# Attention in float32 on one core: two of a chunk's three visits of values' products moved right behind a visit of scores

## Chip, cores, metric

One core of a Trainium2 chip. The metric is the device time of one execution in microseconds (us). Before the change three executions took 698.53, 699.43 and 701.90 us, median 699.43.

## What is computed

```python
# attention: q, k, v are 2 x 12 x 448 x 64 (batch, heads, rows, depth); w_pre, w_post 12 x 12
scores = scale * np.matmul(q, k.transpose(0, 1, 3, 2))
scores = np.einsum('bhij,hg->bgij', scores, w_pre)          # premix over heads
scores = scores - np.max(scores, axis=-1, keepdims=True)
attn = np.exp(scores)
attn = attn / (np.sum(attn, axis=-1, keepdims=True) + 1e-09)
attn = np.einsum('bhij,hg->bgij', attn, w_post)             # postmix over heads
attn_out = np.matmul(attn, v)
# then two feed-forward layers on 896 x 768 tokens (768 -> 2048 -> 768)
g = h * relu6 / 6.0; x = g @ w_out                          # first, h = x @ w_in
g = P / (Q + 1e-06); out = g @ w_out                        # second, P and Q polynomials of h
```

Everything is float32. The two feed-forward layers fill the time from about 225 us on, and the change touches none of their code.

## The kernel before

The 448 query rows of a batch are cut into chunks of 120, 120, 120 and 88 rows (scores are made for 90 of the last), eight chunks over the two batches. A chunk is worked through in **steps** of ten query rows: G = 12 steps in a full chunk, 9 in the last of a batch, 90 steps in all. Counted through, chunk 2 holds steps 24 to 35, chunk 3 holds 36 to 44, chunk 4 holds 45 to 56, chunk 5 holds 57 to 68, chunk 6 holds 69 to 80 and chunk 7 holds 81 to 89. Tiles of a step hold 12 heads times 10 rows on 120 partitions.

Each step m does this:

- `gsplit(m+3)` (L294, L296): GpSimd splits the scores of step m+3 (tile `full`) into a rounded part `sh` and a rest `sl`, three steps ahead.
- `premix(m)` (L306 to L308): three products into bank `M`; VectorE takes the negated maximum (L310), ScalarE the exponential with its row sum (L312).
- `norm`, `weigh` (L320, L321, L325): VectorE takes the reciprocal of the sum, ScalarE scales the postmix weights with it into `wr`. In program order `weigh(m-1)` comes behind the exponential of `premix(m)`, but before it if the step before had a visit (`full_step`).
- `postmix(m-2)` (L341): four products of `e` and `wr` into bank `A`; at the start of the next step ScalarE evacuates them into `at` (L348).

On top of that come **visits** on TensorE. A visit of scores (L271, 12 products, four banks `sc`) makes four heads' scores of the next chunk. Their sums are copied to `stg`, half by ScalarE and half by VectorE (L274), and SyncE spreads them by DMA into `full` (L252), one issue per head. A visit of values' products (`av_unit`, L363, 16 products, one bank `X`) multiplies `at` of the previous chunk with the values `vraw`; its sum goes through ScalarE into `x` or `XH` (L379) and through VectorE into `XL` (L380), and behind a visit SyncE loads the next values into the `vraw` buffers that it freed (L136). A chunk has three visits of either kind. A step without a visit is called a **thin step** below.

The program is recorded in the order of the loop (`tc.manual_schedule`), so each engine runs its instructions in that order. The steps at which visits come are tables: `SST` for scores, `AVST` for values' products.

```python
    SST = {12: [1, 1, 3, 3, 5, 5], 9: [0, 0, 2, 2, 4, 4]}
    AVST = {12: [7, 7, 9, 9, 11, 11], 9: [5, 5, 7, 7, 8, 8]}
            for p in posts[:1] + xposts:
                p[0]()
            gsplit(m + 3)()
            if C:
                for p in posts[:1]:
                    p[1]()
            premix(m)
```

PSUM has two banks `M`, two `A` and four `sc`; bank `X` is one of the four `sc`.

Of the kernel before, what the change touches and what calls it, by code (L numbers as in the profile page):

```python
# [7 lines left out]
F32 = mybir.dt.float32  # L8
# [11 lines left out]
B, H, S, D = 2, 12, 448, 64  # L20
# [28 lines left out]
def fused_kernel(  # L49
# [280 lines left out]
    def postmix(m):  # L330
        C, g = groups[m]
        r, rr = GP, GR
        c0 = row_of(chunks[C], g)
        if g == 0:
            at[C] = att.tile([JP, JC, H, CH], F32, tag="at", bufs=2, name=f"at{C}")
        e, st = epx.pop(m)
        wr = wrs.pop(m)
        A = ps.tile([128, 512], F32, tag="A", name=f"A{m}")
        av = A[:JP, : JC * H * rr].rearrange("p (c h i) -> p c h i", c=JC, h=H)
        for jc in range(JC):  # L340
            nc.tensor.matmul(  # L341
                av[:, jc], lhsT=e[:r, jc * JP : (jc + 1) * JP], rhs=wr[:r, :, :rr], start=True, stop=True
            )
        o = at[C][:, :, :, c0 : c0 + rr]
        if m in BYV:
            aposts.append(lambda: nc.vector.tensor_copy(out=o, in_=av))
        else:
            aposts.append(lambda: nc.scalar.activation(out=o, in_=av, func=AF.Copy))  # L348

    xps = {}  # L350

    def av_unit(C, h):
        b, r0, n, G = chunks[C]
        if h % 2 == 0:
            return
        if h % 4 == 1:
            tag = "sc" if C + 1 < len(chunks) or h == 1 else "A"
            xps[C] = ps.tile([128, 512], F32, tag=tag, bufs=BUFS[tag], name=f"X{C}_{h}")
        X = xps[C][:, : 2 * CH].rearrange("p (h n) -> p h n", n=CH)
        for jc in range(JC):  # L360
            for hh in (h - 1, h):
                vs = vraw[(C, hh // 2)][:, hh % 2, :].rearrange("p (c d) -> p c d", d=D)
                nc.tensor.matmul(  # L363
                    X[hh % 2 * D : hh % 2 * D + D, hh % 4 // 2, :n], lhsT=vs[:, jc, :], rhs=at[C][:, jc, hh, :n],
                    start=(jc == 0), stop=(jc == JC - 1),
                )
        load_v(*((C, h // 2 + 4) if h // 2 + 4 < NP else (C + 1, h // 2 + 4 - NP)))
        if h % 4 == 3:
            av_evac(C, h, X)

    def av_evac(C, h, X):
        b, r0, n, G = chunks[C]
        c0 = (h - 3) // 2
        t0 = b * S + r0
        src = X[:, :, :n]
        cs, ts_ = slice(c0, c0 + 2), slice(t0, t0 + n)
        o = (x1 if t0 < XRAW else XH)[:, cs, ts_]
# [194 lines left out]
    LAG = 2  # L572
    ONES, BYV = [1, 3, 5], (5, 7, 9)


    SST = {12: [1, 1, 3, 3, 5, 5], 9: [0, 0, 2, 2, 4, 4]}
    QST = {12: [8, 9], 9: [6, 7]}
    AVST = {12: [7, 7, 9, 9, 11, 11], 9: [5, 5, 7, 7, 8, 8]}
    VAT = 11
# [6 lines left out]
    for C, (b, r0, n, G) in enumerate(chunks):  # L586
# [6 lines left out]

        sst = SST[G] if C else ONES
        if nxt is not None:
# [9 lines left out]
        if C > 0:  # L605
            add([lambda h=h: av_unit(C - 1, h) for h in range(1, H, 2)], [("av", a) for a in (AVST[G] if nxt is not None else AVLAST)])

        for s in range(G):
# [11 lines left out]
            if full_step:  # L620
                norm(m - 1)
                weigh(m - 1)
            for p in posts[:1] + xposts:
                p[0]()
            gsplit(m + 3)()
            if C:
# [27 lines left out]
            if m >= LAG:  # L654
                postmix(m - LAG)
            for u in sched.get(("av", s), []):
                u()
            for u in sched.get(s, []):
                u()
# [42 lines left out]
    pieces(2)  # L702
    for h in range(1, H, 2):
        av_unit(C, h)
        flush()
# [293 lines left out]
```

## Time and profile before

| | us |
|---|---|
| three executions | 698.53, 699.43, 701.90 |
| the profiled execution | 697.88 |
| span of its profile | 696.1 |
| TensorE busy in it | 686.3 |
| ScalarE busy | 433.8 |
| VectorE busy | 532.7 |
| GpSimd busy | 168.2 |

The profile is of one execution; its span is 1.8 us shorter than its time. Busy times of TensorE are modelled from each product's start, so that products seem to overlap; the distance between starts is the firmer number, and it is used below.

### The profile page before, as it was taken

Reading aid. Unit: us, or ns where it says so; the run is one execution under the profiler, and the core shown is the slowest. Engines: PE = TensorE matmul, PEld = TensorE weight load, DVE = VectorE, ACT = ScalarE, POOL = GpSimd, SP = SyncE. Lnnn points to the kernel's source line nnn. Section 1 sums busy time; section 2 is a strip of 40 time slices with the busy share of each in tenths; the row PEclk is TensorE's granted clock in tenths of the full one; section 3 lists DMA queues with packets and bytes.
Section 4 is the critical chain, followed back from the end, with each engine's and each line's share of the span. In section 5 each row is a group of like instructions: output and inputs, shape, how many; then the busy total and the mean of one; then the engine's idle time right before and its main releaser. Section 6 shows DMA issues by size and latency. Waiting matters only on the chain.

```text
span 696.1 us, 12343 instructions
## 1 busy us (share of the span) xinstructions
PE 686.3 (99%) x4460; PEld 616.2 (89%) x4461; DVE 532.7 (77%) x964; ACT 433.8 (62%) x881; POOL 168.2 (24%) x195
## 2 busy tenths in 40 slices
PE   8999999999999999999999999999999999999998
PEld 4779888888889888989889888898999999999997
DVE  6855685666657699999976556549999899989991
ACT  6767787787887455555543222237766667669851
POOL 2987775877776200000000000000000000000000
PEclk9999999999999999999999999999999999999999
DMA  5646486545394377675743332517666574755522
GB/s 200 232 133 175 138 215 197 163 139 165 120 265 124 113 246 213 199 218 183 230 156 121 121 122 88 184 54 273 212 240 211 180 267 166 243 181 207 190 81 90
DMA packets 76032, 122.81 MB, mean 176 GB/s; under 512 B 6804, under 2 KB 56260, under 8 KB 75972
## 3 DMA queue, kind: packets, MB, share of 16 engines
q1 hardware_dynamic: 75684, 121.66, 54.2%
q8 instruction: 35, 0.57, 0.3%
q10 hardware_dynamic: 288, 0.37, 0.1%
q14 instruction: 25, 0.20, 0.1%
HBM read 83.39 MB, written 19.27 MB: 147 GB/s over the span
## 4 chain that ended last, share of the span: by engine, by line
PE 93%; DMA 2%; DVE 2%; issue 1%; ACT 1%; POOL 0%; SPq 0%; POOLq 0%; DVEq 0%
PE h L389 11%; PE h L388 11%; PE h L387 11%; PE A L341 9%; PE acc L387 6%; PE acc L389 6%; PE acc L388 6%; PE y L388 6%; PE y L387 6%; PE y L389 6%; PE X L363 5%; PE sc L271 4%; PE M L306 3%; PE M L308 2%; PE M L307 2%; DMA vraw<-in_v_dram 1%
## 5 line engine op out<-in xcount | busy, mean ns | idle before, releaser
L389 PE MATMUL h<-xh,wl 128*128 128x512 f32 (+1 forms) x384 | 139.7, 364 | 0.0
L388 PE MATMUL h<-xl,wh 128*128 128x512 f32 (+1 forms) x384 | 139.5, 363 | 0.0
L387 PE MATMUL h<-xh,wh 128*128 128x512 f32 (+1 forms) x384 | 139.5, 363 | 0.0
L296 POOL TENSOR_TENSOR sl<-full,sh 120x448 fp32r<-120x448 f32 x87 | 100.0, 1149 | 7.3
L341 PEld LDWEIGHTS A<-wr,e 120*112 120x112 f32 x720 | 86.4, 176 | 8.0 <-ACT wr L325 4.0
L310 DVE TENSOR_REDUCE st<-M 120x1 f32<-120x448 f32 x90 | 56.0, 622 | 48.2 <-PE M L308 48.1
L341 PE MATMUL A<-wr,e 120*112 120x120 f32 x720 | 88.9, 266 | 2.2 <-ACT wr L325 2.2
L312 ACT ACTIVATE e<-M,st 120x448 f32<-120x448 f32 x90 | 57.1, 635 | 40.5 <-DVE st L310 34.4
L462 ACT ACTIVATE wh<-wf 128x768 fp32r<-128x768 f32 (+1 forms) x52 | 42.6, 819 | 62.0 <-PE y L388 46.6
L387 PEld LDWEIGHTS h<-xh,wh 128*128 128x128 f32 x384 | 72.1, 188 | 7.5
L388 PEld LDWEIGHTS h<-xl,wh 128*128 128x128 f32 x384 | 72.1, 188 | 7.6
L389 PEld LDWEIGHTS h<-xh,wl 128*128 128x128 f32 x384 | 72.1, 188 | 7.6
L435 ACT ACTIVATE wf<-wraw 128x768 f32<-128x768 f32 (+1 forms) x56 | 49.5, 883 | 42.9 <-DVE wl L463 40.8
L463 DVE TENSOR_TENSOR wl<-wf,wh 128x768 fp32r<-128x768 f32 (+1 forms) x52 | 49.6, 954 | 32.4 <-ACT wh L462 32.4
L388 PE MATMUL y<-gl,wh 128*128 128x384 f32 x192 | 70.1, 365 | 0.0
L387 PE MATMUL y<-gh,wh 128*128 128x384 f32 x192 | 69.9, 364 | 0.0
L389 PE MATMUL y<-gh,wl 128*128 128x384 f32 x192 | 69.5, 362 | 0.0
L294 POOL TENSOR_SCALAR sh<-full 120x448 fp32r<-120x448 f32 x87 | 54.0, 620 | 43.5 <-PE M L307 20.6
L443 DVE SCALAR_TENSOR_TENSOR wf<-wraw,icst,wf 128x768 int32<-128x768 int32 (+1 forms) x56 | 56.5, 1011 | 0.7
L439 DVE SCALAR_TENSOR_TENSOR wf<-wraw,icst,wf 128x768 int32<-128x768 int32 (+1 forms) x56 | 55.9, 999 | 0.9
L348 ACT ACTIVATE at<-A 112x480 f32<-112x480 f32 x87 | 50.3, 579 | 1.8 <-PE A L341 1.8
L389 PE MATMUL acc<-ws,xl 128*128 128x384 f32 x128 | 42.8, 334 | 0.0
(115 smaller groups left out, 1416.3 us busy)
## 6 DMA issues: line engine op xcount, KB each, us to landing
wraw<-in_moe_w_out_dram SPq DMA_DIRECT2D x28, 768.0 KB
wraw<-in_moe_w_in_dram SPq DMA_DIRECT2D x22, 768.0 KB
full<-stg SPq DMA_DIRECT2D x60, 210.0 KB
vraw<-in_v_dram SPq DMA_DIRECT2D x42, 224.0 KB
wpre<-in_moe_w_in_dram SPq DMA_DIRECT2D x10, 768.0 KB
w2h<-wh SPq DMA_DIRECT2D x16, 384.0 KB
w2l<-wl SPq DMA_DIRECT2D x16, 384.0 KB
ws<-w2h SPq DMA_DIRECT2D x16, 384.0 KB
```

The source lines that it names most:

```text
L294: eng.tensor_scalar(out=sh[:r], in0=s[:r], scalar1=1.0, scalar2=0.0, op0=ALU.mult, op1=ALU.add)
L296: return lambda: eng.tensor_tensor(out=sl[:r], in0=s[:r], in1=sh[:r].bitcast(F32), op=ALU.subtract)
L310: nc.vector.tensor_reduce(out=st[:r, 0:1], in_=mt[:r, :S], op=ALU.max, axis=AX.X, negate=True)
L312: nc.scalar.activation(out=e[:r], in_=mt[:r, :S], func=AF.Exp, bias=st[:r, 0:1], accum_out=st[:r, 1:2])
L341: nc.tensor.matmul(av[:, jc], lhsT=e[:r, jc * JP : (jc + 1) * JP], rhs=wr[:r, :, :rr], start=True, stop=True)
L348: aposts.append(lambda: nc.scalar.activation(out=o, in_=av, func=AF.Copy))
L387: nc.tensor.matmul(o, lhsT=wh, rhs=mh, start=first, stop=False)
L388: nc.tensor.matmul(o, lhsT=wh, rhs=ml, start=False, stop=False)
L389: nc.tensor.matmul(o, lhsT=wl, rhs=mh, start=False, stop=last)
L439: nc.vector.scalar_tensor_tensor(out=wi, in0=hw, scalar=icst[:, 0:1], in1=wi, op0=ALU.bitwise_and, op1=ALU.bitwise_or)
L443: nc.vector.scalar_tensor_tensor(out=wi, in0=lw, scalar=icst[:, 1:2], in1=wi, op0=ALU.logical_shift_right, op1=ALU.bitwise_or)
L463: nc.vector.tensor_tensor(out=lv, in0=w, in1=hv.bitcast(F32), op=ALU.subtract)
```

## The change

From chunk 2 to chunk 6 (`joint`) the tables change. In a full chunk scores come at steps 1, 3 and 6 (were 1, 3, 5), values' products at 3, 6 and 9 (were 7, 9, 11); in chunk 3, of nine steps, scores stay at 0, 2 and 4 and values' products come at 2, 4 and 7 (were 5, 7, 8). So two of three visits of values' products stand directly behind a visit of scores in the same step (a **joint visit**), and the scores are recorded first there. Their bank is one of the two `A` banks instead of one of the four `sc`. In a joint chunk all copies of scores and of `X`, ScalarE's and VectorE's, are recorded before the step's `premix`. The other edits rename arguments (`hp` for a pair of heads, `wide`) or keep chunks 0, 1 and 7 as they were.

```diff
@@ -342,38 +342,35 @@
                 av[:, jc], lhsT=e[:r, jc * JP : (jc + 1) * JP], rhs=wr[:r, :, :rr], start=True, stop=True
             )
         o = at[C][:, :, :, c0 : c0 + rr]
-        if m in BYV:
+        if (g if C else m) in BYV[C > 0]:
             aposts.append(lambda: nc.vector.tensor_copy(out=o, in_=av))
         else:
             aposts.append(lambda: nc.scalar.activation(out=o, in_=av, func=AF.Copy))
 
     xps = {}
 
-    def av_unit(C, h):
+    def av_unit(C, hp, wide, tag):
         b, r0, n, G = chunks[C]
-        if h % 2 == 0:
-            return
-        if h % 4 == 1:
-            tag = "sc" if C + 1 < len(chunks) or h == 1 else "A"
-            xps[C] = ps.tile([128, 512], F32, tag=tag, bufs=BUFS[tag], name=f"X{C}_{h}")
-        X = xps[C][:, : 2 * CH].rearrange("p (h n) -> p h n", n=CH)
+        i = hp % wide
+        if i == 0:
+            xps[C] = ps.tile([128, 512], F32, tag=tag, bufs=BUFS[tag], name=f"X{C}_{hp}")
+        X = xps[C][:, : wide * CH].rearrange("p (h n) -> p h n", n=CH)
+        vs = vraw[(C, hp)].rearrange("p h (c d) -> p h c d", d=D)
         for jc in range(JC):
-            for hh in (h - 1, h):
-                vs = vraw[(C, hh // 2)][:, hh % 2, :].rearrange("p (c d) -> p c d", d=D)
+            for k in range(2):
                 nc.tensor.matmul(
-                    X[hh % 2 * D : hh % 2 * D + D, hh % 4 // 2, :n], lhsT=vs[:, jc, :], rhs=at[C][:, jc, hh, :n],
+                    X[k * D : k * D + D, i, :n], lhsT=vs[:, k, jc, :], rhs=at[C][:, jc, 2 * hp + k, :n],
                     start=(jc == 0), stop=(jc == JC - 1),
                 )
-        load_v(*((C, h // 2 + 4) if h // 2 + 4 < NP else (C + 1, h // 2 + 4 - NP)))
-        if h % 4 == 3:
-            av_evac(C, h, X)
-
-    def av_evac(C, h, X):
+        load_v(*((C, hp + 4) if hp + 4 < NP else (C + 1, hp + 4 - NP)))
+        if i == wide - 1:
+            av_evac(C, hp - i, hp + 1, X)
+
+    def av_evac(C, p0, p1, X):
         b, r0, n, G = chunks[C]
-        c0 = (h - 3) // 2
         t0 = b * S + r0
         src = X[:, :, :n]
-        cs, ts_ = slice(c0, c0 + 2), slice(t0, t0 + n)
+        cs, ts_ = slice(p0, p1), slice(t0, t0 + n)
         o = (x1 if t0 < XRAW else XH)[:, cs, ts_]
         xposts.append([
             lambda: nc.scalar.activation(out=o, in_=src, func=AF.Copy),
@@ -570,12 +567,14 @@
             aposts.pop(0)()
 
     LAG = 2
-    ONES, BYV = [1, 3, 5], (5, 7, 9)
-
-
-    SST = {12: [1, 1, 3, 3, 5, 5], 9: [0, 0, 2, 2, 4, 4]}
+    ONES, BYV = [1, 3, 5], [(5, 7, 9), ()]
+
+
+    SST = {12: [1, 1, 3, 3, 6, 6], 9: [0, 0, 2, 2, 4, 4]}
+    SST1, AVST1 = [1, 1, 3, 3, 5, 5], [7, 7, 9, 9, 11, 11]
     QST = {12: [8, 9], 9: [6, 7]}
-    AVST = {12: [7, 7, 9, 9, 11, 11], 9: [5, 5, 7, 7, 8, 8]}
+    AVST = {12: [3, 3, 6, 6, 9, 9], 9: [2, 2, 4, 4, 7, 7]}
+    WIDE = 2
     VAT = 11
     AVLAST = [2, 2, 4, 4, 6, 6]
     full_step = False
@@ -591,7 +590,8 @@
             for i, u in enumerate(units):
                 sched.setdefault(steps[i * len(steps) // len(units)], []).append(u)
 
-        sst = SST[G] if C else ONES
+        sst = (ONES, SST1)[C] if C < 2 else SST[G]
+        joint = C > 1 and nxt is not None
         if nxt is not None:
             kw = {} if C else {"first": nc.vector.tensor_copy}
             add([lambda h=h: scores(nxt, h, **kw) for h in range(0 if C else FIRST, NP)], sst)
@@ -603,7 +603,9 @@
         if C == NCH - 1:
             add([lambda h=h: k_prep(1, h) for h in range(4, NP)], [0, 1])
         if C > 0:
-            add([lambda h=h: av_unit(C - 1, h) for h in range(1, H, 2)], [("av", a) for a in (AVST[G] if nxt is not None else AVLAST)])
+            wide = WIDE if joint else 2
+            avst = AVST[G] if joint else AVST1 if nxt is not None else AVLAST
+            add([lambda h=h: av_unit(C - 1, h, wide, "A" if joint else "sc") for h in range(NP)], [("av", a) for a in avst])
 
         for s in range(G):
             if s == (5 if C == 1 else 0) and C and C + 2 < len(chunks):
@@ -620,8 +622,14 @@
             if full_step:
                 norm(m - 1)
                 weigh(m - 1)
-            for p in posts[:1] + xposts:
+            first = posts if joint else posts[:1]
+            for p in first + xposts:
                 p[0]()
+            if joint:
+                for p in first + xposts:
+                    p[1]()
+                posts.clear()
+                xposts.clear()
             gsplit(m + 3)()
             if C:
                 for p in posts[:1]:
@@ -653,9 +661,9 @@
                 next(wpieces)
             if m >= LAG:
                 postmix(m - LAG)
+            for u in sched.get(s, []):
+                u()
             for u in sched.get(("av", s), []):
-                u()
-            for u in sched.get(s, []):
                 u()
             if C == PRE and s == LATE - 1:
                 flush()
@@ -700,8 +708,8 @@
     drain()
     load_units(3)
     pieces(2)
-    for h in range(1, H, 2):
-        av_unit(C, h)
+    for h in range(NP):
+        av_unit(C, h, 2, "sc" if h < 2 else "A")
         flush()
     run(h110)
     h101 = ps.tile([128, 512], F32, tag="M", name="h1_0_1")

```

**TensorE, chunk 2, from the second visit of scores to the third** (`sc` scores, `X` values' products, `M` premix, `A` postmix). Before:

```order
L271 MATMUL sc_7_1181<-xh,qr 90x448
L306 MATMUL M_1202<-sh_1076,wp_h 120x448
L307 MATMUL M_1202<-sh_1076,wp_l 120x448
L308 MATMUL M_1202<-sl_1077,wp_h 120x448
L341 MATMUL A_1214<-wr_1164,e_1135 112x120 x4
L306 MATMUL M_1224<-sh_1123,wp_h 120x448
L307 MATMUL M_1224<-sh_1123,wp_l 120x448
L308 MATMUL M_1224<-sl_1124,wp_h 120x448
L341 MATMUL A_1236<-wr_1192,e_1160 112x120 x4
L271 MATMUL sc_8_1241<-xh,qr 90x448
```

and now, up to the premix of the third step:

```order
L271 MATMUL sc_7_1181<-xh,qr 90x448
L361 MATMUL X_0_1189<-at_720,vraw_0_967 64x120 x8
L361 MATMUL X_0_1189<-at_720,vraw_1_977 64x120 x8
L306 MATMUL M_1229<-sh_1076,wp_h 120x448
L307 MATMUL M_1229<-sh_1076,wp_l 120x448
L308 MATMUL M_1229<-sl_1077,wp_h 120x448
L341 MATMUL A_1237<-wr_1164,e_1139 112x120 x4
L306 MATMUL M_1247<-sh_1129,wp_h 120x448
L307 MATMUL M_1247<-sh_1129,wp_l 120x448
L308 MATMUL M_1247<-sl_1130,wp_h 120x448
L341 MATMUL A_1259<-wr_1213,e_1160 112x120 x4
L306 MATMUL M_1269<-sh_1150,wp_h 120x448
```

The values' products stand behind the scores, and where every second step had a visit, two thin steps now follow each other before the third visit.

**ScalarE, the same place** (`stg` copies of scores, `x` the sum of values' products, `e` exponential, `at` evacuation, `wr` weights). Before:

```order
L274 COPY stg_2_1173<-sc_4_1171 90x448
L312 ACTIVATE e_1208,st_1206<-M_1202,st_1206 120x448
L274 COPY stg_3_1182<-sc_6_1180 90x448
L348 ACTIVATE at_1141<-A_1214 112x48x10
L312 ACTIVATE e_1230,st_1228<-M_1224,st_1228 120x448
L325 ACTIVATE wr_1234<-wq,st_1206 120x120
L348 ACTIVATE at_1141<-A_1236 112x48x10
L325 ACTIVATE wr_1262<-wq,st_1228 120x120
L274 COPY stg_4_1243<-sc_8_1241 90x448
```

and now:

```order
L274 COPY stg_2_1173<-sc_4_1171 90x448
L274 COPY stg_3_1182<-sc_6_1180 90x448
L376 ACTIVATE x_131<-X_0_1189 128x2x120
L312 ACTIVATE e_1235,st_1233<-M_1229,st_1233 120x448
L348 ACTIVATE at_1141<-A_1237 112x48x10
L312 ACTIVATE e_1253,st_1251<-M_1247,st_1251 120x448
L325 ACTIVATE wr_1257<-wq,st_1233 120x120
L348 ACTIVATE at_1141<-A_1259 112x48x10
L312 ACTIVATE e_1275,st_1273<-M_1269,st_1273 120x448
L325 ACTIVATE wr_1279<-wq,st_1251 120x120
L348 ACTIVATE at_1141<-A_1281 112x48x10
L325 ACTIVATE wr_1330<-wq,st_1273 120x120
```

All three copies come ahead of the exponential, and there is one more place at which the weights stand behind the next step's exponential: `wr_1257` behind `e_1253` as `wr_1234` behind `e_1230`, and `wr_1279` behind `e_1275`.

**SyncE, the last spreads of chunk 3** (`full<-stg` spreads one head's scores of chunk 4, `vraw` loads values). Before:

```order
L252 DMA full_1511<-stg_3_1598 10x12x448 x2
L252 DMA full_1511<-stg_4_1660 10x12x448 x2
L252 DMA full_1511<-stg_5_1669 10x12x448 x2
L136 DMA vraw_4_1715<-in_v_dram 112x512
L136 DMA vraw_5_1725<-in_v_dram 112x512
```

and now:

```order
L136 DMA vraw_0_1708<-in_v_dram 112x512
L136 DMA vraw_1_1718<-in_v_dram 112x512
L252 DMA full_1511<-stg_4_1683 10x12x448
L252 DMA full_1511<-stg_5_1692 10x12x448
L252 DMA full_1511<-stg_4_1683 10x12x448
L252 DMA full_1511<-stg_5_1692 10x12x448
L136 DMA vraw_2_1806<-in_v_dram 112x512
```

The four last spreads stand behind two loads of values, which wait for the products of the joint visit.

## Rows read from the trace of the kernel before

**Rows 1.** The page: parts 1 and 2, busy time by engine and TensorE's granted clock.

```profile
PE 686.3 (99%) x4460; PEld 616.2 (89%) x4461; DVE 532.7 (77%) x964; ACT 433.8 (62%) x881; POOL 168.2 (24%) x195
...
PEclk9999999999999999999999999999999999999999
```

**Rows 2.** Timeline of TensorE, steps 57 to 59; start us, us, engine, line, operation.

```profile
145.92 0.46 PE L306 MATMUL M<-sh,wp_h 120*120 120x448 f32 x1
...
146.63 0.98 PE L341 MATMUL A<-wr,e 120*112 120x120 f32 x8
147.38 0.44 PE L306 MATMUL M<-sh,wp_h 120*120 120x448 f32 x1
...
148.05 0.98 PE L341 MATMUL A<-wr,e 120*112 120x120 f32 x8
148.96 0.46 PE L271 MATMUL sc<-xh,qr 64*120 64x448 f32 x2
...
150.07 0.37 PE L271 MATMUL sc<-xh,qr 64*120 64x448 f32 x2
150.37 0.46 PE L306 MATMUL M<-sh,wp_h 120*120 120x448 f32 x1
```

**Rows 3.** Timeline of TensorE, a visit of values' products in chunk 5.

```profile
161.43 0.98 PE L341 MATMUL A<-wr,e 120*112 120x120 f32 x8
162.34 1.86 PE L363 MATMUL X<-at,vraw 112*64 112x120 f32 x32
164.13 0.47 PE L306 MATMUL M<-sh,wp_h 120*120 120x448 f32 x1
```

**Rows 4.** Timeline of ScalarE, step 58: exponential, weights, evacuation, weights.

```profile
148.97 0.64 ACT L312 ACTIVATE e<-M,st 120x448 f32<-120x448 f32 x1 [0.28 <-DVE st L320]
...
149.59 0.38 ACT L325 ACTIVATE wr<-wq,st 120x120 f32<-120x120 f32 x1
...
149.88 0.57 ACT L348 ACTIVATE at<-A 112x480 f32<-112x480 f32 x1
...
150.34 0.38 ACT L325 ACTIVATE wr<-wq,st 120x120 f32<-120x120 f32 x1
```

**Rows 5.** Timeline, step 8 in chunk 0, third of three thin steps in a row.

```profile
30.06 0.37 PE L308 MATMUL M<-sl,wp_h 120*120 120x448 f32 x1
...
30.37 0.38 ACT L325 ACTIVATE wr<-wq,st 120x120 f32<-120x120 f32 x1
...
30.80 1.07 PE L341 MATMUL A<-wr,e 120*112 120x120 f32 x8 [0.38 <-ACT wr L325]
```

**Rows 6.** Timelines of SyncE, TensorE and GpSimd, end of chunk 3.

```profile
110.49 1.61 SPq L252 DMA_DIRECT2D full<-stg  x2
...
114.87 1.13 SPq L136 DMA_DIRECT2D vraw<-in_v_dram  x2
...
115.58 0.18 PEld L306 LDWEIGHTS M<-sh,wp_h 120*120 120x120 f32 x1 [0.16 <-issue]
...
116.86 0.56 POOL L294 TENSOR_SCALAR sh<-full 120x448 fp32r<-120x448 f32 x1 [7.00 <-DMA vraw<-in_v_dram]
...
117.52 1.63 PEld L363 LDWEIGHTS X<-at,vraw 112*64 112x64 f32 x32 [0.44 <-DMA vraw<-in_v_dram]
...
119.48 1.14 POOL L296 TENSOR_TENSOR sl<-full,sh 120x448 fp32r<-120x448 f32 x1
```

**Rows 7.** Timeline, step 36: key conversion on ScalarE, TensorE's wait.

```profile
94.56 1.03 ACT L236 ACTIVATE xh<-kraw 128x448 fp32r<-128x448 f32 x2
...
98.01 0.18 PEld L271 LDWEIGHTS sc<-xh,qr 64*120 64x120 f32 x2 [0.48 <-DVE xh L237]
```

**Rows 8.** Timeline, steps 81 to 83: ScalarE's further work and TensorE's wait.

```profile
201.43 0.90 ACT L435 ACTIVATE wf<-wraw 128x768 f32<-128x768 f32 x1
...
203.81 0.70 ACT L513 CAST xh<-x 128x568 fp32r<-128x568 f32 x1
...
206.27 1.07 PE L341 MATMUL A<-wr,e 120*112 120x120 f32 x8 [0.94 <-ACT wr L325]
```

## Prediction

> **What bounds the kernel now.** I read the page first, then TensorE's own timeline through the 90 steps, then the other engines around it. [...] There [rows 2] a thin step lasts 1.46 us from premix to premix (145.92 to 147.38), of which the postmix takes 0.75 (146.63 to 147.38), and the next step, with a visit of scores, lasts 2.99 (147.38 to 150.37). These two lengths repeat without a wait of TensorE for another engine from step 24 to step 82 except in steps 36 [rows 7] and 44 [rows 6], a step with a visit of values' products being about 0.4 longer. So in the stretch that the change touches TensorE is the bound, and a change there gains only what it takes off TensorE, and loses whatever it makes TensorE wait.
>
> Why does nothing wait? Because thin step and visit alternate. Rows 4 show what the visit covers [rows 4]. In step 58 the exponential starts at 148.97, and only behind it come the weights of step 57, 149.59 to 149.97. That is 2.59 us after the step's premix began (147.38). The postmix that needs them comes after the next premix. With a visit between (148.96 to 150.37 [rows 2]) it comes at about 151.04, 1.1 us after the weights are ready. Without one it would come 2.1 us after that premix (1.46 for the thin step, 0.67 for the premix, 147.38 to 148.05 [rows 2]), half a microsecond too early.
>
> **The change, part by part.**
>
> *Products, copies, loads.* As many as before, on the same engines; only their places move. There are ten joint visits (two in each of chunks 2 to 6).
>
> *Switches of kind on TensorE.* A postmix takes 0.75 us up to a premix but 0.91 up to scores (148.05 to 148.96 [rows 2]) and 0.91 up to values' products (161.43 to 162.34 [rows 3]): 0.16 for entering either kind of visit. Leaving scores costs about 0.10: the last pair of products takes 0.30 to the premix (150.07 to 150.37 [rows 2]), the five pairs before it 0.22 each (148.96 to 150.07). Joining puts one passage from scores to values' products in the place of one leaving and one entering, 0.26 together. No row shows that passage. Its bounds are 0 (saving 0.26) and 0.26 (saving nothing); I take 0.16, as for entering values' products, which is the nearest row. Saving 0.10 each, ten times: **-1.0** (0 to -2.6).
>
> [...]
>
> *Thin steps in a row.* This is the price of joining: the visits no longer alternate. In a full chunk steps 4 and 5, 7 and 8, and 10 and 11 with the next chunk's first are thin in a row. Behind two thin steps the third step's postmix needs weights that stand behind the second's exponential: ready at 2.59 us, wanted at 2.1, so about 0.5 us late. The trace has that very pattern in chunk 0 [rows 5]. The postmix of step 8, third in a row, starts at 30.80, 0.74 after the premix's last product at 30.06, where 0.20 is usual; it is 0.54 late, and the weights (30.37 to 30.75) end just ahead of it. Such steps, apart from the chunks' seams, are 30, 33, 43, 51, 54, 63, 66, 75 and 78: nine times 0.5 is **+4.5** (0.47 to 0.64 each, 4.2 to 5.8).
>
> *The spread of scores at the seams.* Before, scores of chunk 3 were all made by step 40, with four further steps ahead of chunk 4, three of them with a visit. The visits stay there, but the last four spreads now stand behind two loads of values that wait for the joint visit to end, and fewer visits follow. Count from T, the end of that visit. The second load before was issued by 0.4 after the visit (issue ends 116.00, next premix at 115.58 [rows 6]). Four spreads at about 0.85 (two take 1.61, from 110.49 [rows 6]) end at T+3.85. The issue that ended at 112.10 was followed by the split at 116.86, 4.76 later [rows 6]; so `full` is complete at T+8.6. The split takes 0.56 for `sh` and 1.14 for `sl` [rows 6], with 0.1 between, so `sh` is there at T+9.2 and `sl` at T+10.4. TensorE arrives after the steps between. For chunk 4 these are three thin steps and one with values' products (1.45, 1.43, 3.9 with its wait of 0.5, 1.45; 3.4 is 1.46 + 0.16 + 1.79 [rows 2, 3]), T+8.2: 1.0 late at `sh`, then 0.7 at `sl`. For chunk 5 they are four thin ones and a shorter visit, T+9.25: `sl` 0.65 late. For chunk 6, T+9.7, 0.2 late. Then GpSimd needs 1.8 for each further step where thin steps want 1.45, about 0.5 more per seam until a visit comes. Sum 2.2 + 1.15 + 0.7: **+4.1** (2.2, if spreads land a microsecond earlier, to 7.0, if one later). For chunks 3 and 7 the spreads are a quarter smaller and land in time.
>
> *Two seams with other work.* In step 36 TensorE waits 0.48 for key conversions now [rows 7]. Afterwards its postmix is third in a thin run, with one conversion (0.5, half of the 1.03 for two [rows 7]) on ScalarE ahead of the weights: 1.0 late, net **+0.5** (0.3 to 1.0). At steps 81 to 83 ScalarE has more to do, a cast of 0.70 per step and a conversion of 0.90 [rows 8]. With exponential 0.62, weights 0.29 and evacuation 0.46 (spacings in rows 4) two steps cost it 2 x 2.07 + 0.90 = 5.0 where TensorE needs 2.9. It falls 2.1 behind; the visit in step 80 had absorbed half (0.94 of wait is left [rows 8]), and now no visit stands in 79 to 82: net **+1.2** (0.5 to 2.0).
>
> *What goes.* The wait of step 44 for values, at least 0.3 on the weight load's record of 0.44 [rows 6]: **-0.3**, as they are now loaded a visit earlier.
>
> *Bank and copies.* `X` in an `A` bank is read by ScalarE and VectorE within about 0.8 us of the next step's start; the postmix that wants that bank comes 1.45 + 0.67 after it. The copies now ahead of the premix run while TensorE is still in the joint visit. I cost both at 0; cover gone, see the third rival.
>
> Sum: -1.0 + 4.5 + 4.1 + 0.5 + 1.2 - 0.3 = **+9.0 us**. The profiled execution took 697.88, so 706.9 for its like. The median of the runs, 699.43, stands 1.55 above it; against that the forecast is 708.4, 1.3% slower.
>
> **Rivals.**
>
> *The spreads are not late.* SyncE is free at that moment, and the copies are made during the joint visit, so only the loads hold them. If the landing is 1.5 us faster than in the one case read, the 4.1 falls to nothing. For it speaks that less traffic shares the queue then; against it that the 7.00 of GpSimd's wait [rows 6] shows how long it takes even with no load ahead. Then +4.9, 704.3.
>
> *Faster: the passage between visits costs nothing and ScalarE keeps up.* The point from which it decides is 2.1 us from premix to weights. If the weights are there by then, the thin runs are free, -2.6 from switches and -0.3 - 0.48 - 0.94 from old waits would stand alone: 699.4 - 4.3 = 695.1. Rows 4 and 5 speak against it: the order of ScalarE's instructions fixes the 2.59, and step 8 showed the wait. A weak form, in which half the thin runs wait, lands near no change.
>
> *Slower still: the bank.* If the sum of `X` is read later than 2.1 us after the step's start, because two copies of scores stand ahead of it on ScalarE, the postmix two steps on waits. Priced at 0.5 for each of 15 visits, +7.5, 715.9. Against it: those copies wait for nothing but scores that were finished 1.8 us before.
>
> That the change does not move what it says is excluded by the orders shown.
>
> **How the numbers follow.** The forecast has 0.66, spreads in time 0.19, faster 0.07 (0.03 of it the weak form), the bank 0.08. Forecast's own bounds: low ends -2.6 + 4.2 + 2.2 + 0.3 + 0.5 - 0.3 = +4.3, high ends 0 + 5.8 + 7.0 + 1.0 + 2.0 - 0.3 = +15.5. The range 703.5 to 714.0 takes in the first rival and all but the top of those bounds. About 0.5%, 3.5 us, is what a measurement of this kernel can tell from no change. Faster by more: 0.04. Within it: the weak form and the lower end of the first rival, 0.07. Slower: 0.89.
>
> **What would show it.** In the profile after, steps 30, 33, 51 and their like have a wait of the postmix for the weights of ScalarE, 0.3 to 0.6 each. At the seams (steps 45, 57) GpSimd waits for DMA and TensorE for GpSimd. A joint step lasts about 4.85 us without its wait (1.46 + 1.53 + 0.16 + 1.79 - 0.10, [rows 2, 3]). The rest of the program, from 225 us on, is unchanged but for its start. I am wrong if TensorE shows no wait for ScalarE between steps 28 and 80, or if waits show and the joint steps are shorter by as much.

## The result and the profile after

| | before | changed |
|---|---|---|
| median of four runs each, one chip, us | 700.66 | 711.42 |
| lowest and highest, us | 698.53, 703.64 | 710.09, 712.63 |
| the profiled execution, us | 697.88 | 710.27 |
| its span, us | 696.1 | 708.5 |

The ratio is 1.015, with a 95% interval of 1.0102 to 1.0198: slower, by 10.8 us between the medians, and by 12.4 between the two profiled executions. One execution of a later kernel (849.69 us at a mean granted clock of 0.753, the profiled one of the `pa` move) is left out of its ratio, and its steps are not read. The page of the changed kernel, to be set against [rows 1] (the group's columns: busy us, mean ns | idle us just before it and what ended it):

```profile
span 708.5 us, 12302 instructions
...
PE 689.6 (97%) x4461; PEld 615.1 (87%) x4461; DVE 535.0 (76%) x964; ACT 435.7 (61%) x881; POOL 168.4 (24%) x195
...
PEclk9999999999999999999999999999999999999999
...
L341 PE MATMUL A<-wr,e 120*112 120x120 f32 x720 | 90.4, 268 | 8.2 <-ACT wr L325 8.2
```

The same work, the same granted clock, and TensorE at 97 instead of 99%: the time went into waits of TensorE. The view of waits says for whom, over the stretch in which the attention runs (us in total, times, longest):

```profile
PE A L341 <- ACT wr L325: 8.2, 19, 1.0
PE sc L271 <- DVE xh L237: 1.9, 1, 1.9
PE M L308 <- POOL sl L296: 1.5, 2, 0.9
PE M L306 <- POOL sh L294: 1.0, 1, 1.0
```

Before, that first line read 2.2 us in four waits, and the last was there with the same 1.0. The waits as recorded don't give the cost, though, since TensorE's ends are modelled. What gives it is the length of each step, from premix to premix, in both traces. (A **thin run** below is two or more thin steps in a row, a **seam** the passage from one chunk to the next, named by the later chunk.) Steps 24 to 87 took 151.66 us and now take 162.83, 11.2 more. Of the other 1.2 us of the spans' difference, 0.8 lie before step 24 and 0.4 behind step 87, where the change moves nothing; the sum below is for the 11.2.

| steps | before, us | now, us | difference in all | foreseen |
|---|---|---|---|---|
| ten joint visits | 3.47 as two visits' surplus over thin steps | 3.32 (4.77 - 1.45) | -1.5 | -1.0 |
| 30, 63, 75 behind two thin steps | 4.77 to 4.80 (a joint step without a wait) | 5.41 to 5.43 | +1.9 | |
| 51 | 4.37 | 5.01 | +0.6 | |
| 33, 43, 54, 66, 78 | 2.96 to 3.39 | 3.54 to 4.03 | +3.0 | all nine +4.5 |
| 36 | 3.48 | 6.27 | +2.8 | +0.5 |
| 45, 46 | 4.45 | 6.21 | +1.8 | +2.2 |
| 57, 58 | 4.45 | 5.06 | +0.6 | +1.15 |
| 69, 70 | 4.43 | 5.70 | +1.3 | +0.7 |
| 81 to 83 | 7.49 | 8.88 | +1.4 | +1.2 |
| 44's wait for values | 0.34 | none | -0.3 | -0.3 |

Sum 11.5 before rounding; thin steps that are 0.02 or 0.03 shorter than before make up the rest.

One of the nine, in the timeline of the changed kernel, steps 28 to 30 (start us, us, engine, line and operation, idle before and its releaser):

```profile
81.46 0.45 PE L306 MATMUL M<-sh,wp_h 120*120 120x448 f32 x1
81.63 0.64 ACT L312 ACTIVATE e<-M,st 120x448 f32<-120x448 f32 x1 [0.30 <-DVE st L320]
...
82.26 0.38 ACT L325 ACTIVATE wr<-wq,st 120x120 f32<-120x120 f32 x1
82.69 1.07 PE L341 MATMUL A<-wr,e 120*112 120x120 f32 x8 [0.38 <-ACT wr L325]
83.70 0.44 PE L271 MATMUL sc<-xh,qr 64*90 64x448 f32 x2
```

The premix of step 30 begins at 81.46. Its postmix, which usually begins 0.67 us behind that, begins 1.23 behind it, just as the weights of step 28 end (82.64). They stood behind the exponential of step 29. So it is 0.56 late, and it then takes 1.01 to the scores instead of 0.91 [rows 2]: 0.66 together, where the record shows a wait of 0.38.

Step 36, the largest difference, in the timelines of TensorE, GpSimd and VectorE of the changed kernel:

```profile
96.58 0.45 PE L306 MATMUL M<-sh,wp_h 120*120 120x448 f32 x1
...
98.26 1.07 PE L341 MATMUL A<-wr,e 120*112 120x120 f32 x8 [0.82 <-ACT wr L325]
98.78 1.39 POOL L296 TENSOR_TENSOR sl<-full,sh 120x448 fp32r<-120x448 f32 x1
...
99.09 1.10 DVE L183 TENSOR_SCALAR pa<-pa 128x4 f32<-128x4 f32 x1
...
100.11 0.61 DVE L310 TENSOR_REDUCE st<-M 120x1 f32<-120x448 f32 x1
...
100.78 1.13 POOL L296 TENSOR_TENSOR sl<-full,sh 120x448 fp32r<-120x448 f32 x1
...
100.89 2.03 DVE L237 TENSOR_TENSOR xh<-kraw,xh 128x448 fp32r<-128x448 f32 x2
...
102.45 0.47 PE L271 MATMUL sc<-xh,qr 64*120 64x448 f32 x2 [1.90 <-DVE xh L237]
```

TensorE waits twice: for the weights, as foreseen, and then 1.90 us for key conversions. VectorE is late with them: an operation on a tile of 128 x 4 numbers (`pa`) took 1.10 us, and two conversions 2.03. In the trace before, the operation on `pa`, by its line:

```profile
L183 DVE TENSOR_SCALAR pa<-pa x1: 156/156/156, 95.5 to 95.5; 128x4 f32<-128x4 f32 x1
```

156 ns. `pa` ends together with GpSimd's subtraction (at 100.19, the subtraction at 100.17), and the first of the two conversions, 1.50 of their 2.03 us, ends 0.48 behind the next subtraction (at 102.39, the subtraction at 101.91). More on this in the last section. How much of the 2.8 us is due to it varies from kernel to kernel, as the experiments show.

The seam of chunk 4, in the timelines of SyncE, TensorE and GpSimd of the changed kernel:

```profile
114.62 1.14 SPq L136 DMA_DIRECT2D vraw<-in_v_dram  x2
115.33 0.46 PE L306 MATMUL M<-sh,wp_h 120*120 120x448 f32 x1
...
115.85 3.35 SPq L252 DMA_DIRECT2D full<-stg  x4
...
123.06 0.56 POOL L294 TENSOR_SCALAR sh<-full 120x448 fp32r<-120x448 f32 x1 [5.18 <-PE M L307]
...
123.71 1.49 POOL L296 TENSOR_TENSOR sl<-full,sh 120x448 fp32r<-120x448 f32 x1
125.25 0.46 PE L308 MATMUL M<-sl,wp_h 120*120 120x448 f32 x1 [0.90 <-POOL sl L296]
```

The joint visit ends at 115.33. The four spreads stand behind the two loads, their issue ends at 119.20, the split begins 3.86 later, and TensorE waits 0.90 us for the rest `sl`. The releaser named for GpSimd, a premix of TensorE, ended long before 123.06; what it waited for must be the spreads, the last input of that split.

### The profile page after: what moved, and what is told of

Read it like the earlier page. It is cut to its first block, busy times and chain, and to the rows that moved or that the text cites. A ratio compares the mean times of both kernels' runs of the same rounds, so it can differ in the third digit from the quotient of the medians.

```text
span 708.5 us, 12302 instructions
## 1 busy us (share of the span) xinstructions
PE 689.6 (97%) x4461; PEld 615.1 (87%) x4461; DVE 535.0 (76%) x964; ACT 435.7 (61%) x881; POOL 168.4 (24%) x195
## 4 chain that ended last, share of the span: by engine, by line
PE 87%; DVE 4%; DMA 3%; ACT 2%; issue 2%; POOL 1%; SPq 0%; POOLq 0%; ACTq 0%; DVEq 0%
PE h L386 11%; PE h L385 11%; PE h L384 11%; PE A L341 7%; PE acc L384 6%; PE acc L386 6%; PE acc L385 5%; PE y L385 5%; PE y L384 5%; PE y L386 5%; PE X L361 5%; PE sc L271 4%; PE M L306 2%; PE M L308 2%; DVE st L310 2%
## 5 line engine op out<-in xcount | busy, mean ns | idle before, releaser
L341 PE MATMUL A<-wr,e 120*112 120x120 f32 x720 | 90.4, 268 | 8.2 <-ACT wr L325 8.2
```

The costliest lines, as they stand in the source:

```text
L341: nc.tensor.matmul(av[:, jc], lhsT=e[:r, jc * JP : (jc + 1) * JP], rhs=wr[:r, :, :rr], start=True, stop=True)
```

## The experiments

Theory: the thin runs cost through the **order** on ScalarE (weights behind the next exponential), and the seams through the spreads and the conversions. The rivals are ScalarE's load, the loads of values, and the bank and the copies. Unless something else is said, an edit is made to the changed kernel, and a ratio is against the kernel before.

**Weights on VectorE wherever the step before had no visit.**

```diff
-    def weigh(m):
+    def weigh(m, dve=False):
...
-        nc.scalar.activation(out=wr, in_=wq, func=AF.Copy, scale=epx[m][1][:, 3:4])
+        if dve:
+            nc.vector.tensor_scalar(out=wr, in0=wq, scalar1=epx[m][1][:, 3:4], scalar2=None, op0=ALU.mult)
+        else:
+            nc.scalar.activation(out=wr, in_=wq, func=AF.Copy, scale=epx[m][1][:, 3:4])
...
-                weigh(m - 1)
+                weigh(m - 1, joint)
```

> In chunks 2 to 6 the postmix weights of a step that follows a thin step are scaled by VectorE right behind its reciprocal, so they no longer stand behind ScalarE's exponential. Theory (weights behind the exponential cost 0.6 us in each of nine thin runs, and part of the seams of chunks 5, 6 and 7): the nine waits of the postmix shrink to under 0.2 each, the time is 5 to 7 us under the change, about 705. Rival (the late spread of scores, or GpSimd, sets the pace of the thin runs): the time stays within 1 us of the change, about 711, and the waits turn into waits for GpSimd.

It measured 716.20 us, ratio 1.0232 (1.0206 to 1.0257), slower than the change. Timeline of GpSimd, VectorE and TensorE, steps 29 and 30, in this kernel:

```profile
81.74 1.14 POOL L296 TENSOR_TENSOR sl<-full,sh 120x448 fp32r<-120x448 f32 x1
81.82 1.14 DVE L326 TENSOR_SCALAR wr<-wq,st 120x120 f32<-120x120 f32 x1
...
82.88 0.61 DVE L310 TENSOR_REDUCE st<-M 120x1 f32<-120x448 f32 x1
83.10 1.04 PE L344 MATMUL A<-wr,e 120*112 120x120 f32 x8 [0.80 <-DVE wr L326]
```

The scaling began 0.08 us behind GpSimd's subtraction and ended 0.08 behind its end. By its line (ns: least, median, most):

```profile
L326 DVE TENSOR_SCALAR wr<-wq,st x36: 281/868/1271, 71.2 to 217.7; 120x120 f32<-120x120 f32 x36
```

The shortest took 0.28. So the trial doesn't bear on the order, since the weights came no earlier, and step 30 grew to 5.80. What it shows is that the thin runs follow the weights' end, whoever makes them.

**The same with a strided walk through the weights** (heads and rows exchanged in both access patterns, `.rearrange("p h i -> p i h")`), to see whether the walk decides the stretching.

> As the first experiment (weights on VectorE behind the reciprocal), but read and written with heads innermost, so that neighbouring elements are ten apart. There VectorE's scaling took 1.14 us and ended with GpSimd's subtraction beside it. Theory (VectorE's form on neighbouring elements in SBUF waits until GpSimd's instruction ends, the strided form does not): the scaling takes 0.35 us or less, the waits of the nine thin runs shrink to 0.2 or less, and the time is 4 to 6 us under the change, about 706. Rival (VectorE is slow at it anyway, or waits whatever the stride): it takes 0.8 us or more and the time stays near the first experiment's, 714 to 717.

It measured 716.02 us, ratio 1.0236 (1.0197 to 1.0276). By its line:

```profile
L326 DVE TENSOR_SCALAR wr<-wq,st x36: 332/926/1329, 71.2 to 221.8; 120x120 f32<-120x120 f32 x36
```

The walk does not help: the median is 0.93 us.

**The weights ahead of the exponential everywhere in the joint chunks**, on ScalarE as before; one line:

```diff
-            full_step = bool(s in sst if nxt is not None else s >= 7) or ("av", s) in sched
+            full_step = joint or bool(s in sst if nxt is not None else s >= 7) or ("av", s) in sched
```

> One line: in chunks 2 to 6 the reciprocal and the weights of the step before are always recorded ahead of the step's exponential (and of its maximum), as before they were only behind a visit. Theory (the place of the weights behind the exponential costs the nine waits of 0.6 us): the waits of the postmix in steps 30, 33, 43, 51, 54, 63, 66, 75 and 78 go, some 0.1 us per thin step comes back because the maximum now waits for the reciprocal: 4 to 5.5 us under the change, 706 to 707.5. Rival (the thin runs are limited by ScalarE's or VectorE's load, so the order does not matter): within 1.5 us of the change, 710 to 712.

It measured 708.85 us (705.43 to 714.01 in four runs), ratio 1.0138 (1.0085 to 1.019), an interval that overlaps the change's, so by the times alone the gain is not clear of the scatter. The runs' times go with their mean granted clock: 0.997 in the run of 705.43, 0.995, 0.994 and 0.990 in those of 708.65, 709.05 and 714.01 (0.995 to 0.998 in the change's four). So the steps of the profiled execution, the one of 705.43, say more. Steps 24 to 87 take 157.21 us there, 5.6 fewer than with the change. The timeline of ScalarE and TensorE, step 30:

```profile
82.21 0.40 ACT L325 ACTIVATE wr<-wq,st 120x120 f32<-120x120 f32 x1
82.32 0.45 PE L306 MATMUL M<-sh,wp_h 120*120 120x448 f32 x1
...
82.67 0.64 ACT L312 ACTIVATE e<-M,st 120x448 f32<-120x448 f32 x1
...
83.01 0.98 PE L341 MATMUL A<-wr,e 120*112 120x120 f32 x8
...
87.10 0.46 PE L306 MATMUL M<-sh,wp_h 120*120 120x448 f32 x1
```

The weights end at 82.61, 0.29 behind the premix, the postmix begins in its turn, 0.69 behind it, and the step takes 4.78 (5.41 in the change). The same in all nine: 33 takes 3.40, 51 takes 4.37, 78 takes 3.39; none waits. 5.4 of the 5.6 us are these nine. Of the rest, step 36 is 1.0 shorter (but see the queries below), and steps 44 to 46 give 0.9 back: they take 8.58 (7.66 in the change), since TensorE comes there 0.6 earlier and the split begins 4.81 us behind the last spread's issue instead of 3.86.

**The same line in the kernel before**, as a control (`full_step = 1 < C < 7 or ...`).

> The kernel before with the first remedy alone: weights always ahead of the exponential in chunks 2 to 6, no joint visits. Theory (the place of the weights matters only where two thin steps follow each other, and before there is no such place but the seams): no change within 1 us, 699 to 701, no waits in steps 24 to 80 beyond those of before. Rival (the place of the weights gains anywhere): 3 us or more under the kernel before.

It measured 699.67 us, ratio 0.9994 (0.9978 to 1.0011), in ten runs; steps 24 to 87 take 151.9 (151.66 before). The order is worth nothing where visits alternate with thin steps. It costs only in thin runs, and these the change made.

**ScalarE's load.** VectorE takes 15 of the 56 evacuations from step 24 to step 80, three per chunk, among them the one that stands ahead of step 29's exponential and the weights of step 28.

```diff
-        if (g if C else m) in BYV[C > 0]:
+        if (g if C > 1 else m) in BYV[C > 1]:
...
-    ONES, BYV = [1, 3, 5], [(5, 7, 9), ()]
+    ONES, BYV = [1, 3, 5], [(5, 7, 9), (2, 5, 8)]
```

> In chunks 2 to 6 the evacuation of three postmixes per chunk (groups 2, 5 and 8), those that ScalarE does between the two exponentials of a thin run, goes to VectorE. Theory (not ScalarE's load but the place of the weights behind the exponential costs, and that exponential starts when the maximum is there): the waits in thin runs stay at 0.3 us or more by the profile, the time within 1.5 us of the change, 710 to 713. Rival (ScalarE has too much to do in a thin step): it is relieved of 0.46 in a step of 1.45, so the waits of the nine thin runs vanish, 5 us less, 706.

It measured 712.08 us, ratio 1.0168 (1.0143 to 1.0194). Timeline, step 30 of this kernel:

```profile
83.62 0.45 PE L306 MATMUL M<-sh,wp_h 120*120 120x448 f32 x1
...
83.78 0.64 ACT L312 ACTIVATE e<-M,st 120x448 f32<-120x448 f32 x1 [0.78 <-DVE st L320]
...
84.40 0.38 ACT L325 ACTIVATE wr<-wq,st 120x120 f32<-120x120 f32 x1
...
84.83 1.09 PE L341 MATMUL A<-wr,e 120*112 120x120 f32 x8 [0.37 <-ACT wr L325]
```

ScalarE now idles 0.78 us ahead of the exponential, where it idled 0.30, the weights still begin 0.78 behind the premix (0.80 in the change), and TensorE still waits 0.37. (This execution had a mean granted clock of 0.947; against its own joint step without a wait, 4.84, step 30 is 0.62 longer, as in the change.) So the rival of ScalarE's load falls; with the two runs above, the order is shown.

**Scores ahead of the postmix** in a step behind two thin ones, so that the visit covers the weights (`late`), values' products staying behind it.

```diff
+            late = joint and s >= 2 and not any(t in sst or ("av", t) in sched for t in (s - 1, s - 2))
+            for u in sched.get(s, []) if late else []:
+                u()
             if m >= LAG:
                 postmix(m - LAG)
-            for u in sched.get(s, []):
+            for u in sched.get(s, []) if not late else []:
                 u()
```

> Where a joint visit stands behind two thin steps (30, 51, 63, 75) the scores are recorded ahead of the postmix and the values' products behind it, so the visit of scores covers the wait for the weights but is no longer next to the values' products. Theory (the wait is a matter of what covers it): the four waits of 0.6 us go, the saving of about 0.15 at each is lost, 2 us under the change, 709.5; the waits of steps 33, 54, 66, 78 stay. Rival (ScalarE is simply behind, so a wait moved away comes back in the next step): within 0.5 us of the change, 711.4.

It measured 708.03 us, ratio 1.0125 (1.009 to 1.016). Steps 30, 51, 63 and 75 take 4.97, 4.55, 4.98 and 4.96, without a wait, 0.2 more than a joint step; the postmix now parts the two visits, and with that the saving of 0.15 is gone. Steps with values' products alone (33 and its like) stay at 3.97. So cover works as well as order, at the price of the join.

**The tables of before**, with the change's bank and copies kept.

```diff
-    SST = {12: [1, 1, 3, 3, 6, 6], 9: [0, 0, 2, 2, 4, 4]}
+    SST = {12: [1, 1, 3, 3, 5, 5], 9: [0, 0, 2, 2, 4, 4]}
...
-    AVST = {12: [3, 3, 6, 6, 9, 9], 9: [2, 2, 4, 4, 7, 7]}
+    AVST = {12: [7, 7, 9, 9, 11, 11], 9: [5, 5, 7, 7, 8, 8]}
```

> The tables of the steps are those of before, so no visit of values' products shares a step with scores; the bank (one of the two A banks), the order of the copies ahead of the premix and SyncE's order stay as the change has them. Theory (the places of the visits are what costs): back to the time of before within 2 us, 699 to 702, and no thin step follows a thin one except at the seams as before. Rival (the bank taken from the postmix, or the copies ahead of the maximum): most of the loss stays, 706 or more.

It measured 701.97 us in ten runs, ratio 1.0037 (1.002 to 1.0055). Steps 24 to 87 take 153.87, 9.0 fewer than with the change and 2.2 more than before. So the places of the visits are most of the loss. Waits of this kernel over the attention:

```profile
PE X L361 <- DMA vraw<-in_v_dram: 1.4, 2, 1.1
...
PE X L361 <- ACT at L348: 0.7, 2, 0.5
```

The second line is the bank: in steps 56 and 80 a visit of values' products without scores ahead of it waits until ScalarE has evacuated the `A` bank that it wants, and these steps are 0.9 longer together than before. In the change no such wait is listed. The first line is the loads of values: the wait of step 44, as before, and 1.1 for a load that came late in step 35. Why that load was late is not shown.

**Loads of values behind the spreads.** The joint visit's loads are kept in a list and issued when the copies and spreads are.

```diff
-        load_v(*((C, hp + 4) if hp + 4 < NP else (C + 1, hp + 4 - NP)))
+        vload = lambda: load_v(*((C, hp + 4) if hp + 4 < NP else (C + 1, hp + 4 - NP)))
+        if tag == "A" and hp < 4 and C + 1 < len(chunks):
+            vloads.append(vload)
+        else:
+            vload()
...
                 xposts.clear()
+                while vloads:
+                    vloads.pop(0)()
```

> In joint chunks the loads of values behind a joint visit are issued behind the spreads of the same step's scores instead of ahead of them. Theory (the spread is late only at chunk 4's first step): steps 45 and 46, 1.2 and 0.6 us long beyond their like, fall by about 1 to 1.5 us together, nothing else moves, 710. Rival (late spreads carry the seams of chunks 4, 5 and 6, as predicted): 3 to 4 us less, 707.5.

It measured 710.67 us, ratio 1.0144 (1.0119 to 1.017); steps 24 to 87 take 162.98, as in the change. Timelines of SyncE, TensorE and GpSimd, seam of chunk 4:

```profile
115.96 3.35 SPq L252 DMA_DIRECT2D full<-stg  x4
116.15 0.46 PE L306 MATMUL M<-sh,wp_h 120*120 120x448 f32 x1
...
119.41 4.07 SPq L136 DMA_DIRECT2D vraw<-in_v_dram  x4
...
124.84 0.61 POOL L294 TENSOR_SCALAR sh<-full 120x448 fp32r<-120x448 f32 x1 [6.13 <-PE A L341]
```

The loads did hold the spreads back. Counted from T, the end of the joint visit, their issue begins at T-0.19 here (115.96 against 116.15) and at T+0.52 in the change (115.85 against 115.33); at the seams of chunks 5 and 6 it begins at T-1.26 and T-1.70 instead of T+0.52, and the splits there begin 0.6 and 1.2 us earlier. But theory and rival both expected time from it, and none came. At chunk 4 the split begins 5.53 us after the last issue instead of 3.86, at T+8.69 instead of T+7.73, and steps 44 to 46 take 8.29 (7.66). At chunk 5 the split is earlier and TensorE waits for the weights, 0.41 and 0.35, so that steps 57 and 58 take 5.73 (5.06).

**Queries converted a step earlier**, so that VectorE and ScalarE come to step 36 with less.

```diff
-    QST = {12: [8, 9], 9: [6, 7]}
+    QST = {12: [7, 8], 9: [6, 7]}
```

> In full chunks the query conversions come one step earlier (steps 7 and 8 for 8 and 9). Theory (the seams of chunks 3 and 6, 2.8 and 1.3 us, come from VectorE's conversions of queries and keys, which crowd in the thin run at a chunk's end): step 36 shrinks by 1 us or more, steps 69 and 70 by 0.5 or more, 709 to 710. Rival (only the key conversions matter, or they wait for GpSimd whatever stands ahead): step 36 stays within 0.5 us, the time within 0.7 us of the change.

It measured 708.86 us, ratio 1.0137 (1.0105 to 1.0169). Step 36 takes 4.91 (6.27), steps 69 and 70 take 4.99 (5.70): 2.1 us together, and steps 24 to 87 are 1.9 shorter. The wait for keys that is left in step 36 is 0.95, and `pa` takes 1.10 here too.

This can't be put down to the edit. Step 36 also takes 5.03 with evacuations on VectorE, 5.07 with scores ahead of the postmix and 5.79 with the loads behind, and steps 69 and 70 take 4.99 in the last two of these as well, though none of them moves a conversion. Timelines of VectorE and TensorE, step 36, with scores ahead of the postmix:

```profile
99.94 0.53 DVE L183 TENSOR_SCALAR pa<-pa 128x4 f32<-128x4 f32 x1
...
101.16 1.90 DVE L237 TENSOR_TENSOR xh<-kraw,xh 128x448 fp32r<-128x448 f32 x2
...
102.22 0.47 PE L271 MATMUL sc<-xh,qr 64*120 64x448 f32 x2 [0.71 <-DVE xh L237]
```

VectorE's order in this step is the change's, yet `pa` takes 0.53 instead of 1.10 and the wait for keys is 0.71 instead of 1.90. Where VectorE's operations fall beside GpSimd's differs from kernel to kernel, and the length of step 36 with it, by up to 1.2 us.

**Both one-line edits together** (weights ahead, queries earlier).

> Both remedies at once: weights recorded ahead of the exponential in chunks 2 to 6, and query conversions one step earlier. Theory (the thin runs cost 5.5 us and the conversions at the seams about 1.5 to 2, independent of each other): from step 24 to step 88 some 155.5 us, 1.5 under the first remedy alone (157.2) and 4 above the kernel before (151.7), by which the time would be 704 to 706. Rival (both remedies take away the same wait): no shorter than the first remedy alone. It is not expected to beat the kernel before, since the seam of chunk 4 and of chunk 7 stay.

It measured 706.38 us (704.55 to 709.75, six runs), ratio 1.0096 (1.0072 to 1.012). Its profiled execution was its slowest: steps 24 to 87 took 159.21 there, 2.0 more than with the weights alone, with steps 37 and 38 at 2.61 and 5.25 instead of 1.46 and 4.79. There TensorE's granted clock was 0.51. TensorE's busy time and granted clock (the fourth column) in that stretch and behind it:

```profile
104.00:107.00 3.00, 3.00 (x13) 0.51 0.01 3
108.00:117.00 9.00, 9.00 (x100) 1.00 0.60 186
```

These two steps are 1.6 us longer at that clock. Another 1.1 went into steps 33, 54 and 66, where values' products now wait for ScalarE to evacuate their `A` bank (0.33, 0.32 and 0.24 by the record); all other steps together are 0.7 shorter. So whether the two gains add up can't be read from this execution.

**The operation on `pa` moved out of step 36's way.**

```diff
-            if C == 3 and s == 0:
+            if C == 3 and s == 6:
                 build_ab()
```

> The change, with the preparation of two small tables (pa, pb) moved from the first step of chunk 3 to its seventh. In the change's profile VectorE's instruction on pa, 128 x 4 elements, took 1.10 us there and ended with GpSimd's subtraction, against 0.16 before. Theory (it holds up the maximum and the key conversions of step 36): step 36 shrinks by 0.8 to 1.3 us from 6.3, the time by about 1, 710.5. Rival (the key conversions wait for GpSimd by themselves): step 36 stays within 0.4 us.

It measured 709.52 us, ratio 1.0129 (1.0096 to 1.0162). Its step 36 can't be compared, so the trial is inconclusive; hence the same edit with the weights ahead:

> The same move together with the weights ahead of the exponential in chunks 2 to 6. Theory: steps 24 to 88 take 156 to 156.5 us (157.2 with the weights alone), the nine waits stay away, 705 to 706, still 4 to 5 us above the kernel before because of the seams of chunks 3, 4, 6 and 7. Rival (the seam of chunk 3 is a matter of chance between VectorE and GpSimd): steps 36 to 38 come out anywhere within 2 us of those of the weights alone.

It measured 707.68 us (705.35 to 710.28), ratio 1.0095 (1.0061 to 1.0129). Steps 24 to 87 take 158.95. All nine thin-run waits are gone again, as in the first kernel with that line. Step 36 takes 5.13 (5.30 without the move), a difference too small to be put down to the edit; the conversions are stretched all the same (0.98 and 1.68 for two, against 0.61 each alone). Step 46 takes 4.60 here and 3.34 without the move, again at a low granted clock (0.50), behind waits of 0.95 and 0.55 us in step 45:

```profile
126.00:129.00 3.00, 3.00 (x14) 0.50 0.01 3
```

In the first trial, with weights on VectorE, products over 448 columns took 0.57 us in step 37, too, instead of 0.37, and steps 37 and 38 are 1.6 us of that kernel's loss.

No version was faster than the kernel before.

## Why the prediction was right, and where a step of it was not

The forecast was 708.4 and 711.42 was measured: the right side, inside the range, 3 us low. By the sum, +9.0 was foreseen against the 11.2 of the steps that change, and 12.4 between the profiled executions.

- *Thin steps in a row*, +4.5: right and shown. The waits go with the order alone, stay when ScalarE is given less to do, and the order is worth nothing where there are no thin runs. The size was a little low: 0.58 to 0.65 each, +5.5, inside its bounds. The weights came 2.6 us behind the premix of the step before, as worked out; what was left out is that a postmix that waited takes 0.10 longer to the next product.
- *Switches*, -1.0: it was ten times 0.15, -1.5. The passage from scores to values' products costs about 0.11 instead of the 0.16 taken.
- *The seam at step 36*, "net +0.5 (0.3 to 1.0)": the step that failed most, +2.8. It counted one conversion on ScalarE ahead of the weights (a recorded wait of 0.82), and left out VectorE, whose conversions end late beside GpSimd's subtraction (a recorded wait of 1.90). The 2.8 is one execution; three other kernels with the same conversions at the same steps came out 1.6 to 2.3 above the 3.48 of before. That VectorE's lateness makes the wait is seen in the trace; no run took it away, so its cause is argued.
- *The spread of scores at the seams*, "2.2 + 1.15 + 0.7": the sum, 3.6 measured over those three seams, came out near, in part by luck, since the cause holds only at the first. The last issue ended where it was foreseen (T+3.87 for T+3.85), and that SyncE's two loads hold the spreads back is shown by the run with the loads behind. The landing was shorter than in the one case read: 3.86, 3.52 and 3.50 instead of 4.76, about the lower bound of the term and more than half of the first rival's 1.5. So the split began at T+7.7 in chunk 4 where T+8.6 was foreseen, and `sl` alone was late, +1.8; it began at T+7.4 in chunks 5 and 6 and was in time there, as the first rival had it. But these seams still cost 1.9, because TensorE waits for the weights (0.37 in 57, 0.53 and 0.26 in 69 and 70). Of the 7.00 that was held against that rival, 4.76 lay behind the last issue.
- *Steps 81 to 83*, +1.2: it was +1.4. *Step 44*, -0.3: right.
- *Bank and copies*, 0: no wait for the bank is listed in the change, so the third rival falls for its places. With the old tables the bank costs 0.9 of 2.2 us, and it costs again in the kernel with both one-line edits. How much of the change's seams is due to bank and copies stays open.

The faster rival falls with its point: the weights are there 2.6 us after their premix and wanted at 2.1. What the join itself brings is 1.5 us, and 0.3 from step 44, against 13.4 of losses.

## What to carry to other kernels

A bunch of extra work on the busiest engine can be the cover of another engine's chain: before joining two of them, ask what stands under each, and work out when the step behind the longest stretch without one wants its operand. Where an operand then comes late, look at the order on the engine that makes it before its load: here one line of order took away 5.4 us that a quarter of the evacuations taken off that engine did not. And a work item that is moved past a seam meets the seam's other work, on every engine and not only the one that waits.

## What the runs showed of the hardware that was not expected

Three of VectorE's operations, all their operands in SBUF, took longer beside GpSimd's subtraction where that began first, and ended 0.02 to 0.48 us behind its end: scaling weights 1.14 us in the timeline of the first trial (0.08 behind), with 0.28 the least, 0.87 the median and 1.27 the most of 36; `pa`, 128 x 4 numbers, 1.10 in the changed kernel (0.02 behind) and 0.16 before, with no subtraction beside it; a key conversion up to 1.50 in the changed kernel (0.48 behind) and 0.61 at least. The other way round, the subtraction, 1.14 in the median, took 1.39 in step 36 of the changed kernel, where a conversion had begun 0.59 before it. The maximum over a bank of PSUM stays between 0.60 and 0.63 before, in the change and with weights on VectorE, and a reciprocal of one number per partition keeps its 0.16 beside the subtraction. A strided walk did not shorten the scaling (0.93 in the median). Why these operations take longer beside each other no run shows.

How long the four spreads of a seam take is not fixed by the order of issues. In the kernels that issue them as the change does, GpSimd's split begins 3.4 to 5.4 us behind the end of the last issue at the seams of chunks 4, 5 and 6. At the seam of chunk 6, in the change and in the last kernel (SyncE and GpSimd; 3.50 and 5.36):

```profile
173.04 3.35 SPq L252 DMA_DIRECT2D full<-stg  x4
179.89 0.57 POOL L294 TENSOR_SCALAR sh<-full 120x448 fp32r<-120x448 f32 x1 [3.06 <-DMA full<-stg]
...
171.79 3.35 SPq L252 DMA_DIRECT2D full<-stg  x4
180.50 0.57 POOL L294 TENSOR_SCALAR sh<-full 120x448 fp32r<-120x448 f32 x1 [4.91 <-DMA full<-stg]
```

So the 5.53 with loads right behind the spreads is not evidence that these loads delayed them.

TensorE's granted clock fell to 0.51 and 0.50 in the two stretches shown above, and a product over 448 columns took 0.57 us there instead of 0.37. Before the fall TensorE had waited 1.58 us in step 36 (both one-line edits) or 0.95 and 0.55 in step 45 (the last kernel); in the change it waited 1.90 in step 36 and the clock stayed at 1.00, so what decides it stays open.
